# A chunked linear recurrence with a mixture-of-experts layer behind it: scores and outputs in 64 x 64 squares, row stores held back, SyncE's queue in written order

## The chip, the cores and the metric

The kernel runs on one core of a Trainium2 chip. The metric is the device time of one launch in microseconds, the median of three runs. The profile is of one execution, taken by the hardware profiler; times in it count from the start of its span. Engines are named as in the profile: PE (TensorE, matmuls), PEld (TensorE's weight loads), DVE (VectorE), ACT (ScalarE), POOL (GpSimd), SP (SyncE, which here only issues DMAs).

## The reference

The first half is a gated recurrence for each of 4 batches and 8 heads, over 768 tokens, with a state of 48 x 48:

```python
f = 1.0 / (1.0 + np.exp(-f_logit))
for t in range(S):
    state = f[:, :, t, :, None] * state + np.einsum('bhd,bhe->bhde', k[:, :, t], v[:, :, t])
    y[:, :, t] = np.einsum('bhd,bhde->bhe', q[:, :, t], state)
```

The outputs of the heads stand side by side as 3072 rows of 384 numbers. The second half routes each row: the best of 4 groups, then the best of 4 experts in it, each with its softmax weight, and then for that one expert of 16 `out = weight * (relu(x @ w1) @ w2)`, with w1 of 384 x 1024 and w2 of 1024 x 384. All is float32.

## The kernel before, in words

**Units.** The sequence is cut into 6 chunks of 128 tokens, and a chunk's 4 batches into two pairs: 12 units (c, s), each of 2 batches x 8 heads x 128 tokens. A unit passes through these stages:

- load (L563): f_logit, q, k and v come in by one DMA each, 384 KB in pieces of 192 bytes, on SP's queue.
- c, bounded (L572) clamps the gate's logits on DVE. g, gated (L579) makes log gates on ACT (Exp, Ln), sums them along the chunk with a triangular matmul (cs, L595), and takes exp of plus and minus the sums (eq, kh). m, multiplied (L609) puts those factors on q and k. So the decay inside a chunk is carried by q and k, and a chunk is plain products.
- t, turned (L621): 16 transposes on PE, copied by ACT to Tq and Tk.
- s, scored (L643): ap = k q^T for each head, 128 x 128, in two halves of 64 keys against all 128 queries; DVE multiplies by the triangle `tri` (L658) into am.
- n, stated (L661): the sum over the chunk's tokens of k v^T (ds), and on DVE the new state (old + ds) * g.
- w, weighed (L684): y^T = state^T q^T + v^T am in PSUM, copied by ACT to xT.
- d, done (L705): the gate logits of the router from xT. x, listed (L726): xT turned back to rows (x_ps) and stored to x_dram, a table of rows in DRAM, by POOL's queue (ACT's for the last two units).

**Routing.** After each chunk, route (L185), with ACT, PE and DVE in small steps, gives each token a place in its expert's list; it stores each row's weight (meta) beside the row. After chunk 3 (CLOSE) two experts are chosen early: load_early (L740) loads their w1; load_second (L747), a step "u" in the last round, loads their w2; early() (L503) gathers 128 rows each of the first four chunks and runs them beside the end of the recurrence. After the last chunk, choose (L329) names the experts in order of their load and gives the row numbers rows_p; then 16 passes run, each with rows gathered by an indirect DMA on POOL (L402), up (L441), down (L478) and a scattered store (L463). Weights are loaded by SP two or three passes ahead (L393).

**Order.** PE, DVE and ACT run their instructions in the order in which the program writes them (`manual_schedule`, L86). That order is a list of steps: BEGIN (L774) up to unit 2, then for each round i the lists EVEN, ODD or one of ORDERS (L778 to L785). "s" means the next step of unit i's generator `scored`, "x-1" the next step of unit i-1's `listed`, "l+2" the load of unit i+2, "r" the next step of the oldest route, "e" the next of the early passes. SP's DMAs are ordered by the framework's scheduler. Two lists, before:

```python
EVEN = "l+2 d-2 n-1 r r r x-1 x-1 t t t t g+1 g+1 x-1 r s s s s c+2 w d-1 g+2 w g+2 n m+1 m+1".split()
NU: "d-2 r e d-1 x-1 x-1 d-1 x-1 u r r r e e r e r r e r r e r e r r e e e e e".split(),
```

PSUM is one ring of 8 banks (`bank`), taken in turn. Weights have two buffers for w1 and w2 each in pool wp, which stand unused until the early loads, and one each in pool wq, which is opened when the recurrence is over. At the start 32 bf16 matmuls on a constant (L102) keep PE busy before the first data come.

Of the kernel before, what the change touches and what calls it, by code (L numbers as in the profile page):

```python
# [18 lines left out]
P = 128  # L19
# [4 lines left out]
def kernel(  # L24
# [22 lines left out]
    DP = 64  # L47
    KO = DM // P
# [10 lines left out]
    WARM = 32  # L59
# [26 lines left out]
    in_turn.enter_context(tc.manual_schedule(engines={ET.PE, ET.DVE, ET.Activation}))  # L86
# [10 lines left out]
    make_identity(nc, ident)  # L97
    nc.vector.memset(onesb, 1.0)

    idle = bank([P, P], "idle")  # L100
    for _ in range(WARM):
        nc.tensor.matmul(idle, lhsT=onesb, rhs=onesb, start=True, stop=True)  # L102
# [167 lines left out]
    who_too = const([1, EARLY], I32, "who_too")  # L270
# [58 lines left out]
    def choose(sb):  # L329
        number = numbers(sb)  # L330
        mine = sb.tile([P, 2, HP, P], FP32, tag="am", bufs=3, name="mine").rearrange("p r a t -> p (r a t)")[:, 0:2 * GE * GE].rearrange("p (n j e) -> p n j e", j=2, e=GE)
        got = sb.tile([P, GE, 2], FP32, tag="got", bufs=1, name="got")
        for j in range(2):
            nc.vector.tensor_tensor(mine[:, :, j, :], order, number[:, :, j].unsqueeze(1).broadcast_to((P, GE, GE)), OP.mult)
        nc.vector.reduce_sum(out=got, in_=mine, axis=AX)
        nc.vector.tensor_copy(rows_p, got)
        named(GE, sb)
# [179 lines left out]
    with ExitStack() as fast:  # L517
# [7 lines left out]
        for nm, count in (("v", 4), ("eq", 2), ("qh", 3), ("kh", 3)):  # L525
            pads[nm] = [kept([P, 2, H, DP], f"{nm}{i}") for i in range(count)]
        states = [[kept([P, 2, HP, DP], f"st{s}_{i}") for i in range(2)] for s in range(B // 2)]

        def padded():

            for n in range(4):
                for nm in ("eq", "qh", "kh", "v"):
                    if n < len(pads[nm]):
                        nc.vector.memset(pads[nm][n][:, :, :, D:DP], 1.0 if nm == "eq" else 0.0)
                if n == 1:
                    for t in sum(states, []):
                        nc.vector.memset(t[:, :, :, D:DP], 0.0)
                    nc.vector.memset(gw, 0.0)
                if n < 3:
                    yield  # L540
# [4 lines left out]
        NU = len(units)  # L545
        live = {}
# [96 lines left out]
        def scored(i):  # L643
            w = live[i]
            w["am"] = []
            for b in range(2):
                am = sb.tile([P, 2, HP, P], FP32, tag="am", bufs=3, name="am")
                w["am"].append(am)
                ap = [bank([P, HP, P], f"ap{r}") for r in range(2)]
                for a in range(HP):  # L650
                    for r in range(2):
                        rows = slice(DP * r, DP * r + D)
                        for u in range(2):
                            half = slice(u * P // 2, (u + 1) * P // 2)
                            nc.tensor.matmul(ap[r][half, a, :], lhsT=w["Tk"][rows, b, a, half], rhs=w["Tq"][rows, b, a, :], start=True, stop=True)  # L655
                yield
                for r in range(2):
                    nc.vector.tensor_tensor(am[:, r], ap[r], tri.unsqueeze(1).broadcast_to((P, HP, P)), OP.mult)  # L658
                yield

        def stated(i):  # L661
# [3 lines left out]
            if c == NC - 1:  # L665
                return
            old, new = states[s][c % 2], states[s][(c + 1) % 2]
            ds = bank([P, 2, HP, D], "ds")
            for a in range(HP):
                for b in range(2):  # L670
                    for r in range(2):
                        nc.tensor.matmul(ds[DP * r:DP * r + DP, b, a, :], lhsT=w["kh"][:, b, 2 * a + r, :], rhs=w["v"][:, b, 2 * a + r, 0:D], start=True, stop=True)
            yield
            dst = new[:, :, :, 0:D]
            gv = w["g"].unsqueeze(3).broadcast_to((P, 2, HP, D))
            if c:
                sp = sb.tile([P, 2, HP, D], FP32, tag="sp", bufs=1, name="sp")
                nc.vector.tensor_tensor(sp, old[:, :, :, 0:D], ds, OP.add)
                nc.vector.tensor_tensor(dst, sp, gv, OP.mult)
            else:  # L680
                nc.vector.tensor_tensor(dst, ds, gv, OP.mult)
            yield

        def weighed(i):  # L684

            c, s = units[i]
            w = live[i]
            ys = [bank([P, HP, P], f"y{r}") for r in range(2)]
            if c:
                for a in range(HP):  # L690
                    for r in range(2):
                        rows = slice(DP * r, DP * r + D)
                        for b in range(2):
                            nc.tensor.matmul(ys[r][DP * b:DP * b + DP, a, :], lhsT=states[s][c % 2][rows, b, a, :], rhs=w["Tq"][rows, b, a, :], start=(a == 0), stop=False, skip_group_check=True)
            yield
            for a in range(HP):
                for r in range(2):
                    for b in range(2):
                        nc.tensor.matmul(ys[r][DP * b:DP * b + DP, a, :], lhsT=w["v"][:, b, 2 * a + r, :], rhs=w["am"][b][:, r, a, :], start=(c == 0 and a == 0), stop=True, skip_group_check=True)  # L699
            w["xT"] = xT = sb.tile([P, 2, HP, P], FP32, tag="xT", name="xT")  # L700
            for r in range(2):
                nc.scalar.copy(xT[:, r], ys[r])  # L702
# [23 lines left out]
        def listed(i):  # L726
# [3 lines left out]
            x = sb.tile([P, 2, HP, 2, D], FP32, tag="x", name="x")  # L730
# [6 lines left out]
            side(i).dma_start(out=rows_of(c, 2 * s, 2)[:, :, 0:DM], in_=x.rearrange("t b a r d -> t b (a r d)"))  # L737
            yield

        def load_early(pool):  # L740
# [3 lines left out]
            for p in range(EARLY):  # L744
                weights[p] = [load_layer(wp, value(who[0:1, p:p + 1], GE - 1), 1)]

        def load_second():  # L747

            nc.vector.tensor_copy(who_too, who[:, 0:EARLY])
            for p in range(EARLY):  # L750
                weights[p].append(load_layer(wp, value(who_too[0:1, p:p + 1], GE - 1), 2))
# [12 lines left out]
        def advance(gens):  # L764
# [9 lines left out]
        BEGIN = """c0 g0 p g0 g0 m0 m0 m0 m0 l2 t0 t0 t0 t0 c1 g1 g1 s0 s0 s0 s0 g1 g1 p w0 w0 n0 m1 m1 m1 m1 l3 h x0 x0 x0  # L774
            t1 t1 t1 t1 b1 c2 g2 g2 s1 s1 s1 s1 p d0 g2 g2 n0 n1 w1 w1 m2 m2 l4 n1
            d0 x1 x1 t2 t2 t2 t2 c3 g3 g3 x1 s2 s2 s2 s2 w2 g3 g3 d1 w2 n2 m3 m3 c4 g4 g4""".split()
        BEGUN = 3
        EVEN = "l+2 d-2 n-1 r r r x-1 x-1 t t t t g+1 g+1 x-1 r s s s s c+2 w d-1 g+2 w g+2 n m+1 m+1".split()  # L778
        ODD = "l+2 d-2 b n-1 r r x-1 x-1 t t t t g+1 g+1 x-1 r s s s s c+2 w d-1 g+2 w g+2 n m+1 m+1 r n".split()
        ORDERS = {  # L780
            NU - 3: "l+2 d-2 b n-1 r r x-1 x-1 t t t t r g+1 g+1 x-1 r s s s s c+2 w d-1 g+2 w g+2 n m+1 m+1 r n".split(),
            NU - 2: "d-2 r x-1 x-1 r t t t t r g+1 g+1 x-1 s s s s w d-1 w n m+1 m+1".split(),
            NU - 1: "d-2 b r r n-1 x-1 x-1 t t t t r x-1 r s s s s w d-1 w r r".split(),
            NU: "d-2 r e d-1 x-1 x-1 d-1 x-1 u r r r e e r e r r e r r e r e r r e e e e e".split(),
# [3 lines left out]
        def step(nm, i):  # L788
# [6 lines left out]
            elif nm == "u":  # L795
                load_second()
# [250 lines left out]
```

## Time and profile before

| what | value |
|---|---|
| median of 3 runs (lowest, highest) | 435.74 us (435.42, 436.67) |
| the profiled execution's own time, its span | 434.56 us, 432.8 us |
| busy PE, DVE, ACT, POOL | 416.3, 268.0, 155.8, 89.6 us |
| PE on scores, on scores x v, on old states, on state sums | 23.9, 23.5, 10.5, 11.1 us |
| DVE on masks | 48 of 682 ns, 29.8 us |
| first score matmul of units 0 to 11 | 11.76, 22.34, 33.87, 50.06, 61.47, 73.38, 84.25, 95.92, 106.79, 118.37, 129.62, 139.09 us |
| DMA: moved, mean rate | 88.98 MB, 206 GB/s |

A row of the timeline reads: start in us, time it took, engine, line, operation, output <- inputs, shapes, count; in brackets the idle time before it and what ended that. The ends of matmuls are modelled, so what a group really takes is read from its start to the start of the next one. A matmul on f32 data leaves two records, a transpose one.

### The profile page before, as it was taken

Reading aid. Unit: us, or ns where it says so; the run is one execution under the profiler, and the core shown is the slowest. Engines: PE = TensorE matmul, PEld = TensorE weight load, DVE = VectorE, ACT = ScalarE, POOL = GpSimd, SP = SyncE. Lnnn points to the kernel's source line nnn. Section 1 sums busy time; section 2 is a strip of 40 time slices with the busy share of each in tenths; the row PEclk is TensorE's granted clock in tenths of the full one; section 3 lists DMA queues with packets and bytes.
Section 4 is the critical chain, followed back from the end, with each engine's and each line's share of the span. In section 5 each row is a group of like instructions: output and inputs, shape, how many; then the busy total and the mean of one; then the engine's idle time right before and its main releaser. Section 6 shows DMA issues by size and latency. Waiting matters only on the chain. (4 is left out here: it accounts for less than half of the span.)

```text
span 432.8 us, 10251 instructions
## 1 busy us (share of the span) xinstructions
PE 416.3 (96%) x4135; PEld 388.8 (90%) x4135; DVE 268.0 (62%) x781; ACT 155.8 (36%) x341; POOL 89.6 (21%) x135
## 2 busy tenths in 40 slices
PE   8999899999999999699999999999999999999994
PEld 5877788989889896689999999999999999999992
DVE  6564595958897760325099975865865775685240
ACT  5666567666665321121121222222312222231220
POOL 4001121111102017400113213213213112101230
PEclk9999999999999999899999999999999999999998
DMA  9999999999983289966384674875865876685110
GB/s 155 170 187 189 200 198 193 193 194 213 187 301 129 55 283 336 377 253 230 115 292 136 246 256 124 336 218 179 310 208 196 312 232 213 250 300 159 35 43 24
DMA packets 130937, 88.98 MB, mean 206 GB/s; under 512 B 102726, under 2 KB 120876, under 8 KB 130882
## 3 DMA queue, kind: packets, MB, share of 16 engines
q1 hardware_dynamic: 123586, 72.36, 63.9%
q0 software_dynamic: 6688, 15.06, 11.4%
q10 hardware_dynamic: 608, 0.83, 0.6%
q8 instruction: 34, 0.56, 0.6%
q14 instruction: 21, 0.17, 0.1%
HBM read 78.71 MB, written 9.83 MB: 205 GB/s over the span
## 5 line engine op out<-in xcount | busy, mean ns | idle before, releaser
L448 PE MATMUL hp<-xe,w 128*128 128x128 f32 (+14 forms) x864 | 140.7, 323 | 3.5 <-DVE xe L439 3.0
L448 PEld LDWEIGHTS hp<-xe,w 128*128 128x128 f32 x864 | 137.2, 192 | 5.0 <-DVE xe L439 3.2
L488 PE MATMUL yo<-h,w 128*128 128x230 f32 (+13 forms) x672 | 115.8, 333 | 0.0
L488 PEld LDWEIGHTS yo<-h,w 128*128 128x128 f32 x672 | 113.7, 190 | 0.2
L431 DVE STREAM_TRANSPOSE yr<-yT 32x192 f32<-32x192 f32 (+1 forms) x208 | 70.5, 339 | 64.5 <-ACT yT L489 61.9
L449 ACT ACTIVATE h<-hp 128x256 f32<-128x256 f32 (+14 forms) x72 | 34.3, 477 | 109.8 <-PE hp L448 101.8
L424 DVE STREAM_TRANSPOSE xe<-xg 32x192 f32<-32x192 f32 (+1 forms) x208 | 69.7, 335 | 2.9
L463 POOL DMA_INDIRECT out_dram<-yt,xg x32 | 34.5, 1077 | 156.4 <-ACT yt L456 122.4
L489 ACT COPY yT<-yo 128x230 f32<-128x230 f32 (+13 forms) x42 | 13.4, 325 | 80.5 <-PE yo L488 79.1
L402 POOL DMA_INDIRECT xg<-x_dram,rows_p x30 | 29.6, 988 | 51.8 <-DMA out_dram<-yt,xg 28.0
L658 DVE TENSOR_TENSOR am<-ap,tri 128x512 f32<-128x512 f32 x48 | 29.8, 682 | 9.0 <-PE ap L655 9.0
L655 PE MATMUL ap<-Tq,Tk 48*64 48x128 f32 x768 | 23.9, 273 | 0.4 <-ACT Tk L630 0.3
L699 PE MATMUL y<-am,v 128*64 128x128 f32 x384 | 23.5, 273 | 0.2 <-issue 0.2
L655 PEld LDWEIGHTS ap<-Tq,Tk 48*64 48x64 f32 x768 | 20.8, 133 | 2.4 <-issue 1.1
L699 PEld LDWEIGHTS y<-am,v 128*64 128x64 f32 x384 | 21.4, 137 | 1.0 <-DVE am L658 0.5
L595 PE MATMUL cs<-ld_f,tri 128*128 128x384 f32 x48 | 19.5, 531 | 2.5 <-ACT ld_f L589 1.8
L737 POOL DMA_DIRECT2D x_dram<-x x10 | 7.4, 741 | 67.9 <-ACT x L735 67.9
L473 PE MATMUL yo<-w,h 128*128 128x384 f32 x64 | 21.3, 486 | 0.0
L473 PEld LDWEIGHTS yo<-w,h 128*128 128x128 f32 x64 | 11.9, 190 | 7.4
L456 ACT ACTIVATE yt<-yr,xg 128x384 f32<-128x384 f32 (+13 forms) x26 | 14.4, 604 | 5.4 <-DVE yr L431 5.4
L702 ACT COPY xT<-y 128x512 f32<-128x512 f32 x24 | 12.9, 587 | 8.3 <-PE y L699 8.2
L629 PE MATMUL tr_q<-ident,qh 128*128 128x128 f32 x96 | 15.4, 286 | 0.1
(174 smaller groups left out, 394.6 us busy)
## 6 DMA issues: line engine op xcount, KB each, us to landing
w<-in_moe_w_dram SPq DMA_DIRECT2D x34, 1536.0 KB, 8.4
qh<-in_q_dram SPq DMA_DIRECT2D x12, 384.0 KB, 5.4
ld_k<-in_k_dram SPq DMA_DIRECT2D x12, 384.0 KB, 6.9
v<-in_v_dram SPq DMA_DIRECT2D x12, 384.0 KB, 7.4
ld_f<-in_f_logit_dram SPq DMA_DIRECT2D x11, 384.0 KB
x_dram<-x POOLq DMA_DIRECT2D x10, 384.0 KB
x_dram<-x ACTq DMA_DIRECT2D x2, 384.0 KB
out_dram<-yt,xg POOLq DMA_INDIRECT x32
```

Source lines behind the costliest of these rows:

```text
L402: nc.gpsimd.indirect_dma_start(out=w["x"][:, j, :], out_offset=None, in_=x_dram[0:1 + top, :], in_offset=bass.IndirectOffsetOnAxis(ap=rows ...
L424: squares(w, lambda n, k_, rk, g, rg: nc.vector.transpose(out=xT[rg, 0:n, k_], in_=x[rk, 0:n, g]))
L431: squares(w, lambda n, k_, rk, g, rg: nc.vector.transpose(out=y[rk, 0:n, g], in_=yT[rg, 0:n, k_]))
L448: nc.tensor.matmul(hp[:, o, :], lhsT=w1[:, ko, (f + o) * P:(f + o + 1) * P], rhs=w["xT"][:, ko, :], start=(ko == 0), stop=(ko == KO - 1))
L449: nc.scalar.activation(h[:, f:f + 2, :], hp, AF.Relu)
L463: sent = nc.gpsimd.indirect_dma_start(out=out, out_offset=bass.IndirectOffsetOnAxis(ap=w["x"][0:m, j, DM + 1:RW].bitcast(U32), axis=0), in ...
L473: nc.tensor.matmul(yp, lhsT=w["h"][:, fo, :], rhs=w2[:, fo, :], start=(fo == 0), stop=(fo == FO - 1))
L488: nc.tensor.matmul(yp, lhsT=w2[:, fo, m * P:(m + 1) * P], rhs=w["h"][:, fo, :], start=(fo == 0), stop=(fo == FO - 1))
L595: nc.tensor.matmul(cs.rearrange("t h d -> t (h d)"), lhsT=tri, rhs=nl[:, b], start=True, stop=True)
L655: nc.tensor.matmul(ap[r][half, a, :], lhsT=w["Tk"][rows, b, a, half], rhs=w["Tq"][rows, b, a, :], start=True, stop=True)
L658: nc.vector.tensor_tensor(am[:, r], ap[r], tri.unsqueeze(1).broadcast_to((P, HP, P)), OP.mult)
L699: nc.tensor.matmul(ys[r][DP * b:DP * b + DP, a, :], lhsT=w["v"][:, b, 2 * a + r, :], rhs=w["am"][b][:, r, a, :], start=(c == 0 and a == 0) ...
```

## The change

1. **Squares.** scored makes only the two 64 x 64 squares on the diagonal of each head's scores, for both batches in one go (two PSUM banks instead of four, two masks instead of four, with `seen`, the triangle's 64 x 64 corner). The products between the first half's keys and the second half's queries are no longer scores: stated forms the sums of each half (ds0, ds1), and with them a state in the middle of the chunk (mid). weighed takes the first half's outputs from the old state, the second half's from mid, and adds each half's scores x v. All these matmuls have 64 or 48 rows of contraction and 64 output partitions, so each takes one quarter of the array; the halves of an output bank are arranged so that two row halves write different banks (n = r ^ u). In the last chunk the first half's sums are formed as well, where nothing was before.
2. **Order.** The lists are rewritten around it ("s s n w n n ... w n"); the transposes t now come before x-1.
3. **Rows kept.** The rows of units 0 to 7 stay on chip, in the two w2 buffers, and are sent by two DMAs on SP's queue in a new step "o" of round 9, behind the last loads. load_early then loads both layers of the two early experts at once; load_second is gone.
4. **SP in written order.** `manual_schedule` covers SP too.
5. The 32 matmuls at the start are taken out.

```diff
-    in_turn.enter_context(tc.manual_schedule(engines={ET.PE, ET.DVE, ET.Activation}))
+    in_turn.enter_context(tc.manual_schedule(engines={ET.PE, ET.DVE, ET.Activation, ET.SP}))
...
+    seen = const([P, Q], FP32, "seen")
+    for u in range(2):
+        nc.gpsimd.tensor_copy(seen[Q * u:Q * u + Q, :], tri[Q * u:Q * u + Q, Q * u:Q * u + Q])
     nc.vector.memset(onesb, 1.0)
-
-    idle = bank([P, P], "idle")
-    for _ in range(WARM):
-        nc.tensor.matmul(idle, lhsT=onesb, rhs=onesb, start=True, stop=True)
...
         states = [[kept([P, 2, HP, DP], f"st{s}_{i}") for i in range(2)] for s in range(B // 2)]
+        mids = [kept([P, 2, HP, DP], f"mid{i}") for i in range(2)]
...
+        KEPT = NU - 4
...
         def scored(i):
+
             w = live[i]
-            w["am"] = []
+            w["am"] = am = sb.tile([P, 2, 2, HP, Q], FP32, tag="am", name="am")
+            ap = [bank([P, 2, HP, Q], f"ap{r}") for r in range(2)]
             for b in range(2):
-                am = sb.tile([P, 2, HP, P], FP32, tag="am", bufs=3, name="am")
-                w["am"].append(am)
-                ap = [bank([P, HP, P], f"ap{r}") for r in range(2)]
                 for a in range(HP):
-                    for r in range(2):
-                        rows = slice(DP * r, DP * r + D)
-                        for u in range(2):
-                            half = slice(u * P // 2, (u + 1) * P // 2)
-                            nc.tensor.matmul(ap[r][half, a, :], lhsT=w["Tk"][rows, b, a, half], rhs=w["Tq"][rows, b, a, :], start=True, stop=True)
-                yield
-                for r in range(2):
-                    nc.vector.tensor_tensor(am[:, r], ap[r], tri.unsqueeze(1).broadcast_to((P, HP, P)), OP.mult)
-                yield
+                    for u in range(2):
+                        for r in range(2):
+                            rows, cols = slice(DP * r, DP * r + D), slice(Q * u, Q * u + Q)
+                            nc.tensor.matmul(ap[r][cols, b, a, :], lhsT=w["Tk"][rows, b, a, cols], rhs=w["Tq"][rows, b, a, cols], start=True, stop=True, skip_group_check=True)
+            yield
...
         def stated(i):
...
-            if c == NC - 1:
-                return
+            last = c == NC - 1
...
+            ds = [bank([P, 2, HP, D], f"ds{u}") for u in range(1 if last else 2)]
             for a in range(HP):
+                if a == HP // 2:
+
+                    yield
                 for b in range(2):
                     for r in range(2):
-                        nc.tensor.matmul(ds[DP * r:DP * r + DP, b, a, :], lhsT=w["kh"][:, b, 2 * a + r, :], rhs=w["v"][:, b, 2 * a + r, 0:D], start=True, stop=True)
...
+                        for u in range(len(ds)):
+                            rows = slice(Q * u, Q * u + Q)
+                            nc.tensor.matmul(ds[u][DP * r:DP * r + DP, b, a, :], lhsT=w["kh"][rows, b, 2 * a + r, :], rhs=w["v"][rows, b, 2 * a + r, 0:D], start=True, stop=True, skip_group_check=True)
+            yield
             if c:
...
+                nc.vector.tensor_tensor(mid, old[:, :, :, 0:D], ds[0], OP.add)
             else:
-                nc.vector.tensor_tensor(dst, ds, gv, OP.mult)
+                nc.vector.tensor_copy(mid, ds[0])
+            yield
+            if last:
+                return
+            nc.vector.tensor_tensor(new[:, :, :, 0:D], mid, ds[1], OP.add)
+            yield
+            nc.vector.tensor_tensor(new[:, :, :, 0:D], new[:, :, :, 0:D], w["g"].unsqueeze(3).broadcast_to((P, 2, HP, D)), OP.mult)
             yield
...
+            def from_states(u, state):
                 for a in range(HP):
                     for r in range(2):
                         rows = slice(DP * r, DP * r + D)
                         for b in range(2):
...
+                            product(r, u, b, a, state[rows, b, a, :], w["Tq"][rows, b, a, Q * u:Q * u + Q], u == 1 and r == 0)
+
+            def from_scores(r):
+                for a in range(HP):
+                    for u in (1 - r, r):
+                        rows = slice(Q * u, Q * u + Q)
+                        for b in range(2):
+                            product(r, u, b, a, w["v"][rows, b, 2 * a + r, :], w["am"][rows, r, b, a, :], r == 1 or u == 0)
+
+            if c:
+                from_states(0, states[s][c % 2])
+            from_scores(0)
+            yield
+
+            from_states(1, w["mid"])
+            from_scores(1)
...
+            if i < KEPT:
+                if i % 4 == 0:
+                    rows_kept.append(wp.tile([P, FO, DM], FP32, tag="w2", name="x_kept"))
...
+        def send_kept():
+
+            for j, t in enumerate(rows_kept):
+                nc.sync.dma_start(out=rows_of(2 * j, 0, 2 * B)[:, :, 0:DM], in_=t)
...
-            for p in range(EARLY):
-                weights[p] = [load_layer(wp, value(who[0:1, p:p + 1], GE - 1), 1)]
-
-        def load_second():
...
+            es = [value(who[0:1, p:p + 1], GE - 1) for p in range(EARLY)]
+            w1s, w2s = ([load_layer(wp, e, layer) for e in es] for layer in (1, 2))
...
-        EVEN = "l+2 d-2 n-1 r r r x-1 x-1 t t t t g+1 g+1 x-1 r s s s s c+2 w d-1 g+2 w g+2 n m+1 m+1".split()
...
+        EVEN = "l+2 d-2 n-1 r r r t t t t x-1 x-1 g+1 g+1 x-1 r s s n w n n c+2 d-1 g+2 w n g+2 m+1 m+1".split()
+        ODD = "l+2 d-2 b n-1 r r t t t t x-1 x-1 g+1 g+1 x-1 r s s n w n n c+2 d-1 g+2 w n g+2 m+1 m+1 r n".split()
...
+            NU - 3: "l+2 o d-2 b n-1 r r t t t t r x-1 x-1 g+1 g+1 x-1 r s s n w n n c+2 d-1 g+2 w n g+2 m+1 m+1 r n".split(),
```

## The prediction

> **What bounds the kernel now.** I read the busy times by stretch first, because the shares of the whole span (PE 96%) mix three stages. Columns: stretch, then busy us (instructions) of PE, PEld, DVE, ACT and POOL, then granted clock, DMA share, GB/s.
> ```profile
> 20.00:30.00 10.00, 9.14 (x165) 7.74 (x165) 6.44 (x23) 6.41 (x14) 1.31 (x2) 1.00 0.96 189
> 100.00:110.00 10.00, 10.00 (x200) 9.10 (x196) 8.92 (x29) 7.17 (x15) 2.24 (x4) 1.00 1.16 202
> 150.00:160.00 10.00, 9.98 (x100) 9.98 (x101) 8.42 (x33) 2.73 (x8) 0.79 (x1) 1.00 1.00 328
> 300.00:360.00 60.00, 60.00 (x367) 60.00 (x367) 42.93 (x128) 15.43 (x35) 14.93 (x15) 1.00 0.74 254
> ```
> From 181 to 428 us the expert passes keep PE full (60.00 of 60); the change has nothing there, so some 247 us stay. Up to 50 us PE has gaps. From 50 to 145 us it has none, and DVE stands close behind (8.92 of 10).
>
> Next, the waits of the whole span tell who causes the early gaps:
> ```profile
> DVE ld_f L576 <- DMA ld_f<-in_f_logit_dram: 13.2, 9, 3.1
> ```
> DVE is held 13.2 us for gate loads; 2.9 of that lies after 46 us. So the loads pace the first three or four units, then PE does. Scores of units 3, 9 and 11 start at 50.06, 118.37 and 139.09 us (timeline): 68.3 / 6 = 11.4 us a unit, then 20.7 us for two.
>
> Then PE's own timeline, where a start minus the next start is what a group really takes:
> ```profile
> 61.47 1.98 PE L655 MATMUL ap<-Tq,Tk 48*64 48x128 f32 x64
> 63.27 1.05 PE L694 MATMUL y<-Tq,st 48*64 48x128 f32 x32
> 64.25 1.09 PE L714 MATMUL lT<-xT,gw 128*64 128x128 f32 x16
> ...
> 67.33 1.09 PE L672 MATMUL ds<-v,kh 128*64 128x48 f32 x32
> 68.34 0.41 PE L719 MATMUL lg<-fold,lgT 128*128 128x40 f32 x2
> ```
> ```profile
> 142.90 1.92 PE L699 MATMUL y<-am,v 128*64 128x128 f32 x32
> 144.75 0.41 PE L719 MATMUL lg<-fold,lgT 128*128 128x40 f32 x2
> ```
> Each f32 matmul leaves two records. Scores: 64 records in 1.80 us, four quarters side by side, so 16 groups of 0.113. Scores times v: 32 in 1.85, in pairs, 16 groups of 0.116. Old state: 32 in 0.98, 8 groups of 0.122. State sums: 32 in 1.01, 16 pairs of 0.063, though they move only 48 columns.
>
> **The squares on PE.** A group of 128 moving columns takes 0.113 to 0.122; one of 64 columns is in no row. From below: half of it, 0.057. From above: no gain at all, 0.113. The nearest row is the 48-column pair, 0.063, which is more than its columns' share (0.042), so a floor shows there; I take 0.063. Groups after: scores 16, scores times v 16 (twice the instructions, now four abreast), states 16 (8 in chunk 0), sums 16. A middle unit: 64 x 0.063 = 4.03 against 1.80 + 1.85 + 0.98 + 1.01 = 5.64, so 1.61 less. Chunk 0 (2 units): 56 x 0.063 = 3.53 against 4.66, 1.13 less. The last chunk (2 units) now forms a half state that it did not need: 4.03 against 4.63, 0.60 less. Together 8 x 1.61 + 2 x 1.13 + 2 x 0.60 = 16.3 us less of PE's work; at 0.113 it would be 64 x 0.113 = 7.23 a middle unit, 1.6 more.
>
> [...] In short windows of the trace four of the score records start within 0.06 us, though sustained they come every 28 ns. [...]
>
> **DVE and the new chain.** The half state adds a wait: PE's second half of the outputs needs mid, which DVE makes behind two masks.
> ```profile
> 74.52 2.48 DVE L658 TENSOR_TENSOR am<-ap,tri 128x512 f32<-128x512 f32 x4 [2.89 <-PE ap L655]
> 77.27 0.56 DVE L576 TENSOR_SCALAR ld_f<-ld_f 128x768 f32<-128x768 f32 x1 [0.27 <-DMA ld_f<-in_f_logit_dram]
> 77.74 0.95 DVE L615 TENSOR_TENSOR qh<-qh,eq 128x768 f32<-128x768 f32 x1
> 78.61 0.95 DVE L618 SCALAR_TENSOR_TENSOR kh<-kh,ld_k 128x768 f32<-128x768 f32 x1
> ...
> 85.39 1.29 DVE L658 TENSOR_TENSOR am<-ap,tri 128x512 f32<-128x512 f32 x2 [0.37 <-PE ap L655]
> ```
> Masks: two of 0.62 instead of four, 1.24 less a unit. States: two passes of 0.55 become three, 0.55 more. DVE, busy 53.9 of the 70 us from 50 to 120 or 8.8 us a unit, falls to 8.1; PE from 11.4 to 9.8. But the order forms a loop, from the q product of one unit (L615) to the next (durations from the timeline): k product and four transposes at 0.44 each, ready after 2.3; rows' transposes 0.92; prefix sums 1.45; scores 1.0 and 0.2 until DVE sees them, 5.9; on PE in the meantime half the sums, states, first score half and the other sums (0.5 each from 5.7), 7.7, seen at 7.9; mid 0.55, the clamp 0.47, the state's sum 0.55, q product 0.9: 10.4. Behind the waiting PE instructions stand the second outputs and then the next transposes. ACT (46.4 of those 70 us, 7.6 a unit) fits beside it. So I take 10.4, not 9.8: six units save 6 x 1.0 = 6.0 us. Bounds: 0, if another wait restores 11.4, and 9.7 at 9.8. The last two units have no new prefix sums and no clamp, so PE's work counts: 1.61 + 0.60, of which I take 2.0, and 0.5 behind the last scores. Rows' transposes behind q and k cost nothing: they no longer wait for xT, which ACT copies meanwhile; uncovered, 0.9 a unit.
>
> **Stores held back.** What a store costs the loads:
> ```profile
> 65.00:70.00 5.00, 4.82 (x87) 4.43 (x82) 3.40 (x7) 3.29 (x7) 0.00 (x0) 1.00 1.13 169
> 70.00:75.00 5.00, 5.00 (x93) 4.35 (x95) 1.94 (x8) 4.37 (x11) 1.29 (x2) 1.00 1.13 213
> ```
> Without a store 845 KB pass in 5 us; with one 1,065 KB, of which 393 are the store, so 672 of loads: 173 KB or 1.0 us lost. Two stores (21.13 and 33.01 us) stand ahead of the gate load that DVE takes at 45.17 and that holds unit 3: 2.0 us earlier (bounds 0 and 2.4, at the 328 GB/s of weights). In all, loads end some 8 us sooner, near 112, about 9.3 us a unit, which is inside 10.4. The eight then go in two transfers: 3.1 MB, 8 to 10 us, until 121. Behind them on SP's queue: who, two w1 (1.57 MB each, 4.8 us at 328 GB/s), to 131, two w2, which also wait for the transfers that read their buffers, to 141. With all work 10 us earlier, w1 is needed at 138 (148.34 now) and w2 at 150 (159.97 now): slack 7 and 9 us. Without it each us late is one on PE. The early gathers, at 134.76 now, wait for the same transfers: 121 against 124, 3 us of cover. SP in written order: the trace's order already has the loads so; 0, bounds plus or minus 1.
>
> **Warm-up and small edits.** The first prefix sum takes 977 ns where the median is 486, and its four transposes 1.09 us where later ones take 0.60: PE is at half speed after the 32 warm-up matmuls all the same. Removing them: 0; the next gate load holds DVE at 11.5 anyway. [...] The mask copies on POOL and the pads of mid lie beside the first loads: 0.
>
> **The tail.** From 160 to 182 us:
> ```profile
> DVE xe L439 <- DMA xg<-x_dram,rows_p: 9.6, 1, 9.6
> ...
> POOL xg L402 <- DMA w<-in_moe_w_dram: 5.8, 1, 5.8
> ...
> PE hp L448 <- DVE xe L439: 3.0, 1, 3.0
> ```
> The row numbers are ready at 158.8 us, but the gathers start at 161.94: the two w2 loads fill all queues from 150 to 160 (DMA 1.00), and the last weights of the rows land behind them. Then PE stands 3.0 us, and runs at half clock from 181 to 184.5 (0.50 granted at 182 to 184; 1.7 us). With w2 loaded before, gathers start up to 3 us earlier. Bounds: 0 (the next weights collide with the gathers as now) and 4.7; I take 3.0.
>
> **Sum.** 2.0 + 6.0 + 2.5 + 3.0 = 13.5 us off the profiled execution's 434.56 (span 432.8 and 1.8 around it): 421.1. It lies 1.2 below the median of 435.74, so on that 422.2. With the lower bounds together (nothing in the six units, the start or the tail) 433; with the upper ones 435.7 - 2.4 - 9.7 - 2.7 - 4.7 = 416; if small groups go at 0.057, 2 to 4 less.
>
> **Rivals.** *The new wait eats it:* mid or the clamp comes late, units stay near 11.1, and the start and tail give 1 to 2 each: 429. For it: DVE at 8.92 and a written order with no slack; against: PE's sum falls by 1.6. *The quarters take turns:* four loads and four matmuls of 64 columns take as long as four of 128. Place: L655, L672, L694, L699; price 1.6 x 12 = 19 us more, less 5 at both ends: 450. It decides from 5.64 / 64 = 0.088 us a group on; beyond about 0.095 the kernel is slower. For it: 28 ns a record now; against: the pair row, which reaches 0.063 with two, and bursts of four in 0.06. *It does not do what it says:* the loads are paced by their 192-byte pieces, not by stores; then start and tail give 1 and units stay at 10.4: 427.
>
> **Chances.** Forecast (416 to 427) 0.62; wait 0.14; turns 0.13; loads unchanged 0.07; below 416, 0.04. A measurement tells 0.3%, 1.3 us, from no change. Faster by more: 0.62 + 0.04 + 0.07 and most of the wait case, 0.82; same 0.04; slower 0.14. The range, 413 to 434, leaves out the turns and little more.
>
> **What would show it.** L655 64 records in about 1.0 us; scores of units 3 and 9 near 48 and 110.5; last loads issued by 108; w2 landed before 145; no wait of 3 us on xe. Wrong if L699 takes more than 1.4 us a unit, or a PE wait on mid appears.

## The result, and the profile after

The changed kernel takes **469.1 us** (median of four runs, 466.29 to 474.98) where the kernel before takes 435.69 beside it: a ratio of 1.074, 95% interval [1.068, 1.080]. The run of 474.98 was a slow one, over 1.5% above the fastest, and is left out of the ratio. Measured again it was 472.08 against 435.93, 1.081 [1.076, 1.086]. The forecast was 422.2, between 413 and 434, so it was wrong in sign and by 47 us. The profiled execution took 470.01 us with a span of 468.2.

The same four stretches as before, same columns:

```profile
20.00:30.00 10.00, 9.51 (x207) 8.89 (x208) 3.72 (x13) 5.78 (x11) 0.00 (x0) 0.66 1.24 187
100.00:110.00 10.00, 9.15 (x126) 8.50 (x126) 5.32 (x13) 5.57 (x12) 0.00 (x0) 0.66 0.45 84
150.00:160.00 10.00, 10.00 (x231) 8.86 (x229) 5.65 (x19) 6.01 (x13) 2.37 (x3) 0.84 1.02 394
300.00:360.00 60.00, 60.00 (x357) 60.00 (x356) 41.22 (x122) 15.14 (x34) 14.45 (x15) 1.00 0.72 250
```

The expert passes are as they were. In the recurrence three things are new. The granted clock is 0.66 to 0.84 where it was 1.00. DVE is busy 5.3 of 10 us, where it stood close behind PE. And from 100 to 110 us PE starts 126 matmuls, not 200, while the queues are half empty (0.45). So the queues are not the bound, DVE is not, and PE, though shown busy, starts a third fewer matmuls. The scores of units 3, 9 and 11 start at 56.8, 138.9 and 168.5 us (50.1, 118.4 and 139.1 before).

Next, the longest waits of PE from 10 to 180 us (engine, line, waited for: us, times, longest), and what DVE waits for before the half state:

```profile
PE y L701 <- issue: 12.7, 8, 3.5
PE ds L677 <- issue: 9.4, 3, 3.3
```
```profile
DVE mid L680 <- PE ds L677: 20.2, 10, 4.2
```

"Issue" means that the profile shows nothing that PE waited for. DVE waits for PE at mid; PE's matmuls never wait for mid (its weight loads do once, for 0.5 us), and that wait was the prediction's main danger. The timeline of PE shows how such a stop looks:

```profile
67.32 1.16 PE L654 MATMUL ap<-Tq,Tk 48*64 48x64 f32 x64
68.30 0.63 PE L677 MATMUL ds<-v,kh 64*64 64x48 f32 x32
68.75 0.66 PE L701 MATMUL y<-Tq,st 48*64 48x64 f32 x32
69.28 0.69 PE L701 MATMUL y<-am,v 64*64 64x64 f32 x32
69.79 0.28 PE L677 MATMUL ds<-v,kh 64*64 64x48 f32 x6
73.41 0.66 PE L677 MATMUL ds<-v,kh 64*64 64x48 f32 x26 [3.33 <-issue]
```

The scores go in 0.98 us (68.30 - 67.32), as forecast. But in the middle of the second half of the state sums, after 6 of 32 matmuls, whose operands had long been there, 3.55 us pass to the next start. Number all the instructions of PE that the trace records (matmuls, weight loads and, between them, semaphore instructions) in one row by their start, from 0. Between 12 us and the first early pass, a distance of more than 0.3 us from one start to the next stands ahead of 15 of the numbers 193 + 256k: 449, 961, 1473, 2241, 2753 and so on; together 27.2 us. Two of the 15 are no stops but the usual distance of the wide prefix-sum matmuls, 0.32 us each. The kernel before has two in all, 0.8 us together. PE has other waits at other numbers, but those over 0.7 us are 5.4 us together. On the DMA queue named "instruction" (q8) the page lists packets, MB and share; each of these packets has 16,384 bytes in both traces, which is 64 bytes an instruction if it holds 256. Before, then after:

```profile
q8 instruction: 34, 0.56, 0.6%
```
```profile
q8 instruction: 43, 0.70, 0.7%
```

In the stop shown, such a packet moved from 70.32 to 71.78 us, and PE went on at 73.41. All 13 stops of the change at these numbers end so, 1.2 to 1.7 us after a packet has come in. And behind some stops the clock goes down (columns as in the first table):

```profile
70.00:75.00 5.00, 1.67 (x47) 1.45 (x42) 0.96 (x3) 0.00 (x0) 0.00 (x0) 0.97 0.72 104
75.00:80.00 5.00, 5.00 (x82) 4.54 (x79) 3.22 (x8) 3.48 (x7) 0.00 (x0) 0.50 0.37 76
```

Between 12 and 190 us the clock is at half for 37.5 us in all (3.4 before).

**Theory.** PE runs out of instructions: they come in blocks of 256, a block takes some 4 us to come (an estimate; e4 below shows 3.73), and squares of 64 columns use one up in 1.9 us (1.87 in e4). **Rivals:** the held stores, SP's order or the missing warm-up did it; the new wait for mid; the squares themselves cost more than their columns.

### The profile page after: what moved, and what is told of

Read it like the earlier page. It is cut to its first block, busy times and chain, and to the rows that moved or that the text cites. A ratio compares the mean times of both kernels' runs of the same rounds, so it can differ in the third digit from the quotient of the medians.

```text
span 468.2 us, 12470 instructions
## 1 busy us (share of the span) xinstructions
PE 418.5 (89%) x5255; PEld 388.2 (83%) x5255; DVE 261.5 (56%) x772; ACT 156.8 (33%) x341; POOL 84.6 (18%) x129
## 5 line engine op out<-in xcount | busy, mean ns | idle before, releaser
L657 DVE TENSOR_TENSOR am<-ap,seen 128x512 f32<-128x512 f32 x24 | 15.5, 686 | 25.8 <-PE ap L654 25.8
L596 PE MATMUL cs<-ld_f,tri 128*128 128x384 f32 x48 | 20.5, 547 | 8.0 <-ACT ld_f L590 6.8
L701 PE MATMUL y<-am,v 64*64 64x64 f32 x768 | 18.8, 233 | 7.9 <-issue 7.6
L677 PE MATMUL ds<-v,kh 64*64 64x48 f32 x704 | 16.2, 217 | 9.4 <-issue 9.4
L677 PEld LDWEIGHTS ds<-v,kh 64*64 64x64 f32 x704 | 14.1, 135 | 12.4 <-issue 12.4
L630 PE MATMUL tr_q<-ident,qh 128*128 128x128 f32 x96 | 20.6, 354 | 0.5 <-DVE qh L616 0.3
L701 PEld LDWEIGHTS y<-am,v 64*64 64x64 f32 x768 | 15.5, 145 | 6.5 <-issue 6.0
L603 POOL DMA_DIRECT2D ends<-eq x10 | 5.4, 543 | 80.2 <-ACT eq L597 80.2
L630 PE MATMUL tr_k<-ident,kh 128*128 128x128 f32 x96 | 19.3, 340 | 0.2 <-DVE lgs L748 0.2
L596 PEld LDWEIGHTS cs<-ld_f,tri 128*128 128x128 f32 x48 | 8.6, 204 | 11.8 <-POOL blank L174 5.8
```

The lines of the kernel that those rows point to most:

```text
L596: nc.tensor.matmul(cs.rearrange("t h d -> t (h d)"), lhsT=tri, rhs=nl[:, b], start=True, stop=True)
L630: nc.tensor.transpose(out=pt[:, a, :], in_=w[nm + "h"][:, b, 2 * a:2 * a + 2, :].rearrange("t r d -> t (r d)"), identity=ident)
L677: nc.tensor.matmul(ds[u][DP * r:DP * r + DP, b, a, :], lhsT=w["kh"][rows, b, 2 * a + r, :], rhs=w["v"][rows, b, 2 * a + r, 0:D], start=Tru ...
L701: nc.tensor.matmul(ys[n][DP * b:DP * b + DP, r, a, :], lhsT=lhsT, rhs=rhs, start=(n, b) not in begun, stop=last, skip_group_check=True)
```

## The experiments

The runs lay on several chips. The kernel before takes 429 us on some and 436 on others, so times are compared as ratios to the kernel before on the same chip, with 95% intervals. From one kind of chip to the other even ratios need care: the filler has 1.098 and 1.096, but e2 has 1.007 where before takes 429 and g2, which differs from it by eight tiny transfers, 0.993 where it takes 436. "Stops" are counted as above, as number and us. The last column runs from the start of PE's last matmul.

| run | us (before beside it) | ratio to before | stops | half clock, 12 to 190 us | from PE's last matmul to the span's end |
|---|---|---|---|---|---|
| before (profile) | | 1 | 2, 0.8 | 3.4 | 6.2 |
| the change | 469.10 (435.69) | 1.074 [1.068, 1.080] | 15, 27.2 | 37.5 | 12.4 |
| the change, again | 472.08 (435.93) | 1.081 [1.076, 1.086] | 15, 27.2 | 47.8 | 12.4 |
| e1 matmuls cut in two | 462.06 (429.13) | 1.077 [1.069, 1.084] | 12, 23.7 | 13.7 | 6.3 |
| e3 squares alone | 456.10 (429.13) | 1.063 [1.055, 1.070] | 13, 23.2 | 30.7 | 6.2 |
| e2 all but the squares | 432.91 (429.13) | 1.007 [1.004, 1.010] | 1, 1.0 | 0 | 12.4 |
| fl filler | 469.91 (429.14) | 1.098 [1.094, 1.102] | 8, 7.6 | 6.8 | 12.4 |
| fl2 filler, beside "again" | 477.10 (435.93) | 1.096 [1.091, 1.101] | 9, 8.4 | 3.4 | 12.4 |
| s1 another order | 473.92 (429.14) | 1.102 [1.096, 1.108] | 11, 19.3 | 20.5 | 12.4 |
| d1 no squares, rows at once | 427.31 (429.14) | 0.996 [0.995, 0.998] | 2, 2.1 | 0 | 6.2 |
| f1 rows held, POOL sends | 433.22 (429.14) | 1.009 [1.006, 1.012] | 3, 3.1 | 10.2 | 6.2 |
| g1 2,048 pieces | 437.23 (436.08) | 1.002 [1.000, 1.004] | 2, 0.8 | 13.7 | 6.3 |
| g2 eight transfers | 433.18 (436.08) | 0.993 [0.991, 0.995] | 1, 0.7 | 0 | 13.3 |
| h1 = d1 and warm-up | 431.09 (436.08) | 0.987 [0.985, 0.989] | 2, 1.2 | 3.4 | 6.5 |
| v1 = e2 and spread pieces | 429.11 (435.93) | 0.985 [0.981, 0.988] | 1, 0.5 | 0 | 6.2 |
| v1w = v1 and warm-up | 426.52 (435.93) | 0.979 [0.976, 0.983] | 1, 0.3 | 0 | 6.5 |

**The same work in twice the instructions (e1).** The kernel before, with each matmul of 128 columns as two of 64, in the scores and in both products of the outputs:

```diff
-    nc.tensor.matmul(ap[r][half, a, :], lhsT=..., rhs=w["Tq"][rows, b, a, :], ...)
+    for h in (slice(0, 64), slice(64, 128)):
+        nc.tensor.matmul(ap[r][half, a, h], lhsT=..., rhs=w["Tq"][rows, b, a, h], ...)
```

> The kernel before, with its order, stores, warm-up and waits untouched; only each matmul of 128 moving columns in the scores, the old states' outputs and the scores' outputs is issued as two of 64 columns, one behind the other. The columns that pass are the same 5.64 us a middle unit, the instructions about 64 matmuls (256 records of PE and its weight loads) a unit more, some 2,900 in all on top of 8,270. Theory 'PE runs out of instructions': PE stands with nothing awaited every 256 records in these groups, 1 to 4 us each time, and the granted clock falls behind some of the stops: 25 to 45 us slower, 460 to 480. Rival 'the change's new wait, order or stores did it': none of them is in here, so 0 to 4 us slower, 436 to 440. Rival 'quarters of 64 columns cost as much as of 128': the groups in the trace take 0.11 us each and there are no stops.

1.077: as slow as the change, with nothing of it in the kernel. Its timeline of PE has the stop in the old states' outputs, at number 2241:

```profile
51.94 2.10 PE L656 MATMUL ap<-Tq,Tk 48*64 48x64 f32 x128
53.86 0.63 PE L696 MATMUL y<-Tq,st 48*64 48x64 f32 x29
58.76 1.33 PE L696 MATMUL y<-Tq,st 48*64 48x64 f32 x35 [4.27 <-issue]
```

The cut scores take 1.92 us (53.86 - 51.94) where the uncut take 1.80: here the columns set the time of a group, and the number of instructions sets the stops (12, 23.7 us, where the kernel before has 2 and 0.8).

**The change taken apart (e2, e3).** e2 has the change without scored, stated, weighed and their lists; e3 has those alone on the kernel before.

> The changed kernel with the squares undone: scores, states and outputs and their order as before; the rows of eight units kept on chip, their two stores, SP's written order and the missing warm-up stay. Theory 'PE runs out of instructions': PE has its 8,270 records again, no stops with nothing awaited beyond those of before, clock 0.99, and the parts that stay give what little they can: 428 to 436. Rival 'held stores, SP's order or the warm-up did it': it stays near 469, at least above 450.

> The kernel before with the squares and their order lists alone; the stores go unit by unit, SP is ordered as before and the warm-up stays. Theory 'PE runs out of instructions': the same stops each 256 records and the same half clock: 460 to 478. Rival 'held stores, SP's order or the warm-up did it': the squares' saving of PE columns shows, 422 to 432.

The squares carry 1.063 (456.10 us, somewhat less than the 460 that I took as the least), the rest 1.007; together 1.070, and the change, on other chips, has 1.074 and 1.081. The rivals of the held stores, SP's order and the warm-up fall for the bulk of the loss. Yet e2 is no gain on its chip, though its stops are gone but for 1.0 us; what ate the gain is in the last column of the table, and comes below.

**The supply by itself (e4).**

> A probe that computes nothing of the reference: four stretches of 512 f32 matmuls of 64x64 quarters (2,048 records of PE and its weight loads each). Stretch 1 moves 64 columns and no data are loaded beside it; stretch 2 the same beside 16 loads in 192-byte pieces; stretch 3 the same beside 24 loads in large pieces; stretch 4 moves 128 columns beside small pieces. Theory 'PE runs out of instructions': a group of four of 64 columns needs 58 ns and so 256 records 1.9 us, but stretch 1 shows a stop at each 256 records so that a block lasts 4 us or more, 30 to 40 us for the stretch in place of 15; if the loads delay the instruction blocks, stretch 2 lasts longer than 1 (5 us a block), and 3 lies between; stretch 4 needs 3.7 us a block by its columns and so shows short stops or none. Rival 'no limit of instructions': each of the stretches 1 to 3 lasts about 15 to 18 us, with no stops, and 4 about 30.

Its timeline in the first stretch, with no data moved:

```profile
10.22 2.09 PE L31 MATMUL b<-x 64*64 64x64 f32 x128 [1.36 <-issue]
13.95 2.09 PE L31 MATMUL b<-x 64*64 64x64 f32 x128 [1.64 <-issue]
17.68 2.09 PE L31 MATMUL b<-x 64*64 64x64 f32 x128 [1.64 <-issue]
```

Each run is 128 matmuls and 128 weight loads, 256 instructions, to the record, and the next starts 3.73 us after it. Without the stop they take 1.87, by their starts. The trace shows the packets in between: in this stretch one begins to move 1.1 to 1.5 us after PE has begun a block, moves for 0.9 to 1.4 us, and PE goes on 1.2 to 1.4 us after its end. So in this stretch a packet moves only when PE is already 1.1 to 1.5 us into a block, and the three steps one behind the other are the 3.7 us. The four stretches (columns: stretch, then busy us and instructions of PE, PEld, DVE and POOL, clock, DMA share, GB/s), each of 2,048 records or eight blocks:

```profile
0.70:29.00 28.30, 18.28 (x1018) 17.48 (x1021) 0.48 (x1) 0.00 (x0) 1.00 0.02 4
29.00:62.00 33.00, 20.48 (x1030) 19.30 (x1025) 0.37 (x3) 0.00 (x0) 0.84 0.86 172
62.00:100.00 38.00, 21.82 (x1052) 20.52 (x1044) 0.37 (x3) 0.00 (x0) 0.82 0.85 271
100.60:134.30 33.70, 30.98 (x1024) 29.71 (x1024) 0.06 (x1) 0.00 (x0) 0.95 0.86 172
```

A block takes 3.5 us on the average with the queues empty (28.30 / 8; 4 or more was expected), 4.1 beside loads in 192-byte pieces and 4.75 beside large pieces, the last two partly at half clock (0.84 and 0.82). That the large ones are the worst was a miss: I had put them between. The fourth stretch moves twice the columns and takes 33.7 us where the second took 33.0, 4.2 a block: twice the columns in the same number of instructions cost 0.7 us more in the stretch, at a granted clock of 0.95 against 0.84.

The kernel before has 0.8 us of such stops in all. The probe and the change have more: with matmuls of 64 columns the crossing from one block to the next costs 1.9 us with idle queues (3.73 - 1.87) and up to 3.7 in the profile of the change (145.0 to 148.7 us).

**Work added where PE would stand (fl, fl2).** One needless f32 matmul before the scores, one before the state sums, one before the outputs; here the first:

```diff
+    nc.tensor.matmul(ap[0].rearrange("p b a i -> p (b a i)"), lhsT=ident, rhs=w["kh"][:, 0].rearrange("p h d -> p (h d)"), start=True, stop=True, ...)
```

> The changed kernel with work added that nobody needs: one f32 matmul of 512 or 384 columns (four records of PE and its loads, 0.54 us for 384 columns in the trace, so some 0.72 for 512) before the scores, one before the state sums and one before the outputs of each unit; its result is overwritten. That is 1.98 us of PE a unit, 24 us in all, and 12 records a unit more. Theory 'PE runs out of instructions': the added work stands where PE would stop, so the stops shrink and the clock holds better: the ratio to before lies between 1.05 and 1.09, at most 8 us over the changed kernel. Rival 'PE's own work is the bound': 24 us more, 1.12 to 1.14.

> The kernel with the three fillers a unit again, now on the same chip as the changed kernel. In the first trace a filler of 512 columns took 1.06 us and one of 384 columns 0.85, so the three are 2.97 us a unit and 36 us in all. Theory 'PE runs out of instructions': at most 10 us over the changed kernel, a difference of the ratios under 0.024. Rival 'PE's work is the bound': 36 us more, a difference of 0.08.

> The changed kernel itself, unaltered, to stand beside the filler on one chip: 1.070 to 1.082 of before.

The fillers take about 1.05, 0.85 and 1.05 us by their starts, 36 us in all, and the kernel is 5.0 us slower on the same chip (477.10 against 472.08; ratios 1.096 and 1.081). On the first chip 1.098 lay above the range that I gave (1.05 to 1.09), and below the rival's. The waits of PE in the changed kernel, then with the fillers:

```profile
PE y L701 <- issue: 12.2, 8, 4.1
PE ds L677 <- issue: 8.8, 3, 3.3
```
```profile
PE y L704 <- issue: 3.9, 6, 1.0
PE lT L745 <- issue: 2.2, 1, 2.2
```

Stops fall from 27.2 to 8.4 us and the half clock from 47.8 to 3.4. 31 of 36 us of work fitted into time in which PE had nothing to run or ran at half speed. Were PE's own work the bound, all 36 would show.

**Another order of the same instructions (s1).** Scores in two halves between transposes and prefix sums, rows' transposes and routing between the other dense groups:

```diff
-EVEN = "l+2 d-2 n-1 r r r t t t t x-1 x-1 g+1 g+1 x-1 r s s n w n n c+2 d-1 g+2 w n g+2 m+1 m+1".split()
+EVEN = "l+2 d-2 n-1 r t t g+1 s t t g+1 s s r n x-1 r w n n x-1 c+2 d-1 x-1 g+2 w r n g+2 m+1 m+1".split()
```

> The changed kernel, the same instructions on PE, in another order: the scores are issued in two halves between the q and k transposes and the prefix sums, and the transposes of the rows and two steps of the routing stand between state sums, first outputs and second outputs, so that PE's runs of 512 small records without anything else become runs of 128 to 256. Theory 'PE runs out of instructions': the stops get fewer and shorter and the clock falls less often; the ratio to before goes from 1.074 to between 0.99 and 1.04. Rival 'it is the number of instructions alone that counts' (each 256 cost the same wherever they stand): 1.06 to 1.08. Rival 'the new order costs DVE more than it gives': PE waits on am or mid appear.

A miss: 1.102, no faster than the change. The stops did fall (27.2 to 19.3 us), and so did the half clock (20.5). But the order put new waits of PE elsewhere:

```profile
PE cs L596 <- ACT ld_f L590: 8.8, 5, 5.8
PE y L701 <- issue: 6.7, 5, 2.8
PE tr_q L630 <- DVE qh L616: 3.9, 4, 1.2
PE rk L209 <- DVE ohe L204: 3.1, 3, 1.0
```

Waits of over 0.7 us away from the block's edge (12 to 185 us) were 5.4 us together in the change and are 19.7 here. 5.8 us of the first line are at the start, as in the change. The third theory of that expectation is near: PE does wait for DVE, but for the q product and the routing; for am it waits 0.3 us in all, for mid not at all. Whether an order exists that spreads the instructions without such waits was not tried further.

**The closing (d1, f1, g1, g2, v1).** e2's last matmul started at 417.9 us, but its span ended at 430.4. The last work in the timeline of before, then of the change, with the span of each:

```profile
core 0 of [0], span 432.8 us
...
428.28 1.00 POOL L463 DMA_INDIRECT out_dram<-yt,xg  x1 [7.33 <-DVE yt L460]
```
```profile
core 0 of [0], span 468.2 us
...
457.49 0.99 POOL L461 DMA_INDIRECT out_dram<-yt,xg  x1 [7.33 <-DVE yt L458]
```

4.5 us follow the start of the last store before, 10.7 in the change. The trace lists there POOL's closing drain: 1.86 us before, 6.77 in the change and in e2, and an update of POOL's DMA counter ahead of it of 0.50 and 1.84. The data of the last store have landed 2.4 to 2.5 us after its start in both.

> The changed kernel without the squares and without the held rows: each unit's rows are sent at once as before; what stays of the change is SP's written order, the order of the early weights and the missing warm-up. The run without squares showed the scores 3.5 us earlier and PE's end 8.6 us earlier than in the profile of before, but its last POOL instruction, the closing drain, took 6.77 us where the kernel before shows 1.86, and the counter update ahead of it 1.84 for 0.50. Theory 'the closing follows what POOL stored': POOL issues its ten row stores again and the drain is 1.9 us; the ratio to before is 0.997 to 1.004. Rival 'SP's order or the warm-up lengthens the closing': the drain stays at 6.8 and the ratio is 1.007 to 1.02.

> The changed kernel without the squares; the rows of eight units are held on chip as in the change, but POOL sends them in its two transfers in place of SP. Theory 'the closing follows how many pieces POOL stored': they are as many as before (8 units of rows), so the drain is 1.9 us and the ratio to before 0.985 to 0.997. Rival 'it follows the number of POOL's DMA instructions' (two in place of eight): the drain stays over 5 us, 1.002 to 1.010. Rival 'POOL's queue cannot take them there': the first gathers come later than without the squares and PE waits for xe.

```diff
-KEPT = NU - 4
+KEPT = 0                     # d1
-nc.sync.dma_start(out=rows_of(2 * j, 0, 2 * B)...)
+nc.gpsimd.dma_start(out=rows_of(2 * j, 0, 2 * B)...)   # f1
```

With rows sent at once the drain is 1.87, and with two large transfers on POOL 1.75: so it follows POOL's share of the stores, not the held rows. f1's time, 1.009, has another cause: POOL sent the first held rows at 55.6 us, in the middle of the loads, and units 5 and 9 came 3.9 and 9.2 us later than in e2.

> The changed kernel without the squares, rows held and sent by SP, and one more transfer on POOL that nobody needs: 2,048 pieces of 4 bytes (16 words of each partition, apart from each other) behind the first three gathers of the expert passes. So POOL has as many pieces to send as in the kernel before, where eight stores more of 256 pieces each stand in its queue. Theory 'the closing follows the number of pieces that POOL sent': the closing drain falls from 6.77 to about 1.9 us and the counter update from 1.84 to 0.50, the rest stays, so 6 us off the run without squares: a ratio to before of 0.990 to 0.997. Rival 'it follows the number of POOL's transfers or the bytes': the drain stays at 6.77 and the ratio at 1.005 to 1.010.

> As the run with 2,048 pieces, but eight transfers of 16 pieces of 4 bytes each, so that POOL issues as many transfers as in the kernel before with only 128 pieces more. Theory 'pieces': the drain stays at 6.77 us, ratio 1.005 to 1.010. Rival 'number of transfers': the drain is 1.9 us, ratio 0.990 to 0.997.

```diff
+    extra = dp.tile([P, GE, 2], U32, name="extra")
+    nc.gpsimd.dma_start(out=extra[:, :, 0:1], in_=rows_p[:, :, 1:2])     # g1: 2,048 pieces
```

2,048 pieces of 4 bytes in one transfer: 1.78. Eight transfers of 16 pieces: 7.42. So in these runs the number of pieces that POOL has sent decides, not the number of transfers. It is not simply that more pieces shorten the drain: 128 more lengthened it, 2,048 more shortened it. g2's ratio, 0.993, lies outside the range that went with the right theory; its chip is one of 436, and e2's was one of 429. g1 paid for the pieces elsewhere: between the first `down` matmul of the early passes and the next `up`, 21.5 us passed in place of e2's 10.6, 8.6 of them a wait of PE, and 10.2 us ran at half clock. Spread over eight expert passes they cost less:

> The changed kernel without the squares, rows held and sent by SP, and POOL's 2,048 pieces of 4 bytes put back as eight transfers of 256, one beside each of eight expert passes from the third on, where the queues are less full than at the first gathers. Theory 'the closing follows the pieces that POOL sent, and the pieces themselves cost nothing there': PE's end as without squares (418 in a trace with 272 us of expert passes), drain 1.9 us in place of 6.77: 5 to 7 us under the run without squares, a ratio to before of 0.975 to 0.993 depending on whether the kernel before waits for its first gathered rows on this chip. Rival 'the pieces delay the gathers there too': PE waits for xe in the expert passes and the ratio is over 1.000.

> The same kernel with the 32 warm-up matmuls put back, on the same chip. Theory 'the warm-up bought nothing': within 0.3% of the run without it. Rival 'it was worth something': at least 0.4% faster than without it, with the granted clock full earlier than 10 us or units that start over 1 us earlier.

```diff
+        if 2 <= n < 10:
+            nc.gpsimd.dma_start(out=extra[:, 2 * n:2 * n + 2, 0:1], in_=w["x"][:, 0, 0:4].rearrange("p (a b) -> p a b", b=2)[:, :, 0:1])
```

v1: drain 1.81 and 0.985; beside g2, also measured where before takes 436, the ratio is 0.8% lower. With the warm-up put back as well, v1w: 426.52 us against 435.93, **0.979 [0.976, 0.983]**, on that chip faster than both kernels. On a chip of 429 it was not measured.

**The warm-up (h1, v1w).**

> The changed kernel without squares and without held rows (ratio 0.996), with the 32 warm-up matmuls put back. What is left of the change is SP's written order and that of the early weights. Theory 'the warm-up bought nothing' (the clock is granted no earlier with it): 0.994 to 0.998, first scores within 0.3 us of those without. Rival 'the warm-up delays or helps the first unit': more than 0.3% from 0.996, and the first scores move by 1 us or more.

h1 and d1 lay on different chips, so their ratios (0.987, 0.996) do not settle it. v1 and v1w lay on one: 429.11 (428.68 to 430.16) without, 426.52 (425.92 to 427.69) with, 0.6% apart. In these two traces the full clock is granted at 11.6 us without and at 9.3 with it, the first scores start at 12.5 and 12.0, those of unit 5 at 70.2 and 68.4. That the warm-up brings the clock earlier is not shown: over all traces of these kernels it comes at 9.2 to 11.6 us without and at 5.0 to 10.5 with it. Half a microsecond is the first unit's; where the other two come from these runs do not show.

## Why the prediction was wrong, point by point

- **The size of the squares: right.** Taken: 0.063 us a group of four. Measured: scores 0.98 us (16 groups, 0.061), in dense runs 0.058. The bound of 0.113 and the rival "the quarters take turns" fall. In e4 256 records, 128 of them matmuls, pass in 1.87 us, 15 ns a matmul record, where the uncut scores have 28 (1.80 us for 64).
- **The step that failed** is "PE from 11.4 to 9.8 ... so I take 10.4". It summed the time that PE's groups take and the chain of waits, and took it that the instructions are there. Their supply was the third bound. Before, a middle unit has some 436 records (955 of PE and 957 of its loads between 70 and 120 us, by 11.4 of 50 us); the squares add 48 matmuls of four records, 192, so 628. At 4.1 us a block (e4's second stretch) that is 628 / 256 x 4.1 = 10.1 us if spread evenly, and the squares stand in runs of 512 records that take 4.0 us and need 8.2. The kernel before had dense blocks too, the shortest of 4.2 us: it stood at the edge, so that doubling instructions for half the columns went straight over it.
- **The price of a stop** came twice in the change: its length, and behind some of them the half clock. Of the 48.9 us between the forecast for the profiled execution (421.1) and its 470.0, the added stops are 26.4, half of the added 34.1 us at half clock is at most 17.1, and the closing is 6.2: 49.7 together. That this comes so near is in part luck: it takes the forecast's other gains as had, and the runs without the squares show them only in part.
- **The wait for mid:** the prediction let the chain through mid set the pace (10.4 us a unit, not 9.8) and named a wait of PE for mid as a sign of being wrong. No such wait came, but that is no merit: PE itself was later, and DVE waited 20.2 us for it there. How far the chain would bind is not shown.
- **Stores held back (2.0), SP's order (0):** the sum was near, the parts were not. The gate load of unit 3 is taken at 45.2 us before, at 41.7 in d1 with SP's order and no held rows, at 40.5 in e2; scores of unit 3 at 50.1, 46.8 and 47.1. So most of it came with SP's written order (d1 lacks the warm-up too), and the held rows bring about 1 us by unit 11 (136.9 and 135.6). These traces are of different chips.
- **Six units 6.0 us:** without the squares the loop goes at 11.3 us a unit (e2: 114.8 - 47.1 over six), so nothing else would have brought it.
- **The tail (3.0):** in e2, as in d1, PE no longer waits for xe (3.0 us before, 1.9 in the change), and the early passes start 1 to 2.5 us sooner. But no step of the sum went behind PE's last matmul, and 6.2 us came there; on e2's chip they outweigh what was won (1.007).
- **The warm-up (0):** mis-sized; 2.6 us on the one chip that compares it, by a path that is not shown.
- **The rival on the slow side** was 450 by quarters in turn. The sign that it had was right, and its mechanism was not: nothing in the prediction counted instructions, though the 34 instruction packets stood on the page.

## What to carry to other kernels

Count TensorE's instructions beside its columns: in e4 256 matmuls and weight loads in a dense run of 64 columns needed 3.5 to 3.7 us to come, 4.1 beside 192-byte loads and 4.75 beside large ones, so in this kernel, by an estimate from these figures, splitting matmuls can pay only where that many still take longer. An idle time that ended at "issue", at equal distances in the count of instructions (13 stops of the change, at the numbers 193 + 256k), was the sign of it; added work that hardly lengthened the run (fl2: 36 us of work, 5.0 us longer) told it from a bound by PE's own work. And the time between the last matmul and the end of the span (6.2 us before, 12.4 in the change) belongs into the sum.

## What the runs showed of the hardware that was not expected

- Instructions of PE come in blocks of 256: 3.5 to 3.7 us from block to block with nothing else moved, 4.0 to 4.3 beside 192-byte loads, 3.5 to 5.9 beside large ones (e4, 64 columns, from the first stop on).
- In the change's trace the granted clock goes to 0.5 for 3.4 or 6.8 us at 74.7, 102.0, 129.3 and 149.8 us, 1.0 to 1.3 us after stops of 3.2 to 3.7 us have ended. A stop of 2.2 us (41.1 to 43.3) was also followed by 3.4 us at half clock, at 44.0, and one of 1.3 us (17.7 to 19.0) by 6.8, at 20.1, while a wait of 2.7 us for a DMA (49.4 to 52.1) was followed by none. So the length of the stop alone does not tell whether the clock falls.
- POOL's closing drain: 1.75 to 2.15 us in the runs with 2,048 more pieces on POOL's queue, 6.77 in those without, 7.42 with 128 pieces in eight transfers more (g2). What the drain does with them stays open.
- The first pass over gathered rows lasts 15.1, about 17.5 or 20.4 to 20.8 us between its first and last matmul of `up`, in traces of kernels alike in it. On chips where before takes 429 us every trace has 15.1; where it takes 436, g1 and g2 have 15.1, v1 and v1w 17.5, and before, the change, fl2 and h1 the longest. It may be what sets the two kinds of chip apart; there is no trace of the kernel before on a chip of 429, so that is not shown.
